# A two-layer decode kernel: the product of probabilities and values with V as the moving operand in four column tiles, its diagonal blocks summed under masks

## The chip, the cores and the metric

The kernel runs on one core of a Trainium2 chip. The metric is the device time of one execution in microseconds (us). Three runs of the kernel before gave 1208.24 us as their median (1208.14 to 1208.75).

## The reference, cut to what matters

Eight sequences (b) of one token each pass through attention, an MLP, the same attention with the same weights and caches, and the same MLP. The caches are read twice, once per layer, since layer 1's queries depend on layer 0's result.

```python
# x [8,1,512]; k_cache, v_cache [8 b, 8 kv heads, 8192 keys, 128]; wq [512,4096]; wo [4096,512]
q = (layernorm(x) @ wq)                       # 32 query heads of 128, four per kv head
scores = einsum("bhqd,bhkd->bhqk", q, k) * 128**-0.5
p = softmax(scores)
o = einsum("bhqk,bhkd->bhqd", p, v)
x = x + o.reshape(8, 1, 4096) @ wo
x = x + silu(layernorm(x) @ w1) @ w2          # w1 [512,1792], w2 [1792,512]
# and the same two blocks once more
```

## The kernel before, in words

**Tasks.** One task is the attention of one layer, one b and one kv head g: 8192 keys and four queries (`REP`). There are 2 x 8 x 8 = 128 tasks, in an order that `make_tasks` (line 141) writes out. Layer 0 of every b comes before layer 1 of the same b. Between them lies a chain of dense work on the token b: output projection, residual, layer norm, MLP, residual, layer norm, query projection for layer 1.

**Granules, halves and positions.** A task has four granules (k = 0 to 3) of 2048 keys, and each granule two halves. A granule of K or V is one load of 512 KB into one of 27 slots of the tile `arena`; partition p holds 16 successive keys, 128 elements each. The program steps through positions p, eight per task (one per half). I call p mod 8 the phase: task i has its scores at positions 8i to 8i+7, its softmax at phases 0 to 7 of the next task's positions, and its PV at positions 8i+13, 15, 17 and 19 (`LP` = 12 positions behind).

**Kept slots.** The last 18 of the 32 (g, k) pairs keep their transposed K in its slot from layer 0 to layer 1 (`KEEP`). In layer 1 the heads g = 4 to 7, and half of g = 3, then load only V. I call these the kept tasks of layer 1. The transposed K of a granule takes the place of K in its slot.

**Loads.** `plan_loads` (line 172) sorts the loads by the position that needs them and gives each a slot and the position after which that slot is free. SP issues them in that order (`issue_until`, line 394; `issue`, line 352; the DMA at line 334), each behind a wait for the PE work that last used the slot. Where slots change hands fastest, in the tasks between the kept ones, a load is issued 7 or 8 positions before it is needed; in the kept tasks of layer 0, 16 to 25 positions.

**One position, in the order in which the program emits it (from line 748).** Every engine executes its own instructions in that order.

- `emit_q` (line 449), once a task: ACT copies the task's queries into QB.
- `emit_t` (line 424): PE transposes the eight 128x128 chunks of the half two positions ahead (line 433). An evacuation copies the result from PSUM back into the slot: three of eight on ACT (line 439), five on DVE (line 441).
- At odd phases `emit_s` (line 458), the scores of the granule: four matmuls with 512 columns each, one in each column tile of 32 (line 464). The queries are the weights and K^T moves. A column tile holds 16 rows in use: four queries times four granules.
- At odd phases `emit_pv` (line 526), both halves of the granule 12 positions back: 16 matmuls with a 128x128 chunk of V as weights and the four columns of P^T, each repeated 12 times, as the moving operand (line 537).
- Softmax. Phase 0: row maxima on DVE (L475), spread onto a diagonal (L477). Phase 1: an fp32 matmul with ones (L485) hands the maxima to all rows; DVE forms the shift (L488, L491), ACT the exponential P and its row sums (L495). Phase 3: sums (L501 on DVE, L504 on POOL). Phase 4: PE transposes P (L513), DVE copies it into PT (L517). Phase 7: reciprocal (L524).
- One or two pieces of the chain, or one head's part of the output projection (`add_heads`, line 709).
- At phase 4, `emit_norm` (line 544, DVE at L551): the task's output times the reciprocal.

PSUM has two banks for scores (SCp), two for PV (OTp), three for transposes (TPp) and one for the dense work (MISC). The bank OTp of a task also takes L485's result.

## Time and profile before

| what | value |
|---|---|
| median of three runs | 1208.24 us |
| the profiled execution's own time | 1207.81 us |
| its span, first to last instruction | 1205.7 us |
| granted TensorE clock, mean | 0.977 |
| PE, DVE, ACT, POOL busy | 981.2, 611.8, 386.1, 70.8 us |
| instructions | 45853, of them 20216 matmuls and 20216 weight loads |
| HBM read | 473.44 MB, 393 GB/s over the span |
| instruction fetches (queues q8 and q14) | 2.61 and 0.32 MB |
| loads of V and K | 512 and 368, 512 KB each |
| issue to landing, median | V 10.7 us, K 15.1 us |

PE is the TensorE, DVE the VectorE, ACT the ScalarE, POOL the GpSimd; SP only issues transfers. The busy time of an engine is an average over stages with different limits, so what counts is the stage: the tables by window show it. "L464" is line 464 of the kernel. In the chain of waits, each step is followed back to what released it; "issue" is time in which the engine waited for nothing that the profile shows. The two microseconds between the execution's time and its span lie outside the first and last instruction.

### The profile page before, as it was taken

How to read it: one execution, taken by the hardware profiler on the slowest of the kernel's cores; microseconds unless marked ns; L12 is line 12 of the kernel's file. 1: busy time of each engine (PE TensorE's matmuls, PEld its weight loads, DVE VectorE, ACT ScalarE, POOL GpSimd, SP SyncE). 2: the span in 40 equal slices, each digit the busy share in tenths (PEclk: the TensorE clock that was granted, in tenths of full speed). 3: DMA queues.
4: the chain of work that ended last, by engine and by line, in shares of the span. 5: the costliest groups of instructions: out<-in, count | busy, mean ns of one | idle time of the engine just before them, and what ended most of it. 6: DMA issues, size and time to landing. Idle time of an engine off the chain costs nothing.

```text
span 1205.7 us, 45853 instructions
## 1 busy us (share of the span) xinstructions
PE 981.2 (81%) x20216; PEld 772.2 (64%) x20216; DVE 611.8 (51%) x1853; ACT 386.1 (32%) x670; POOL 70.8 (6%) x172
## 2 busy tenths in 40 slices
PE   2868898778888788878888898788888898889885
PEld 2656675667666676667666676667666675667564
DVE  2534564446445554546454554446454554456443
ACT  1323332333233332333233332333233333333231
POOL 0000000000000000000000000000000000000000
PEclk7889999999999999999999999999999999999996
DMA  9999999999999999999999999999999999999994
GB/s 370 385 398 408 403 405 406 408 406 399 396 408 408 408 371 404 408 407 403 399 408 407 405 378 408 409 407 395 385 408 407 401 402 407 408 404 398 390 408 172
DMA packets 133926, 476.43 MB, mean 395 GB/s; under 512 B 14160, under 2 KB 20064, under 8 KB 133216
## 3 DMA queue, kind: packets, MB, share of 16 engines
q1 hardware_dynamic: 133728, 473.51, 99.6%
q8 instruction: 159, 2.61, 0.9%
q14 instruction: 39, 0.32, 0.1%
HBM read 473.44 MB, written 0.01 MB: 393 GB/s over the span
## 4 chain that ended last, share of the span: by engine, by line
DMA 47%; PE 32%; DVE 11%; issue 5%; SPq 3%; ACT 2%; POOL 0%; POOLq 0%; ACTq 0%; DVEq 0%
DMA arena<-in_A_k_cache_dram 45%; PE TPp L433 9%; PE OTp L537 9%; PE SCp L464 5%; PE MISC L613 5%; DVE arena L441 3%; SPq L334 3%; DMA arena<-in_A_v_cache_dram 2%; ACT P L495 2%; PE OTp L485 2%; PE TPp L513 1%; DVE rowmax L475 1%; DVE PT L517 1%; PE MISC L631 1%; DVE tr L593 1%
## 5 line engine op out<-in xcount | busy, mean ns | idle before, releaser
L441 DVE COPY arena<-TPp 128x1024 bf16<-128x1024 bf16 x460 | 317.1, 690 | 384.0 <-PE TPp L433 383.6
L433 PE MATMUL TPp<-ident,arena 128*128 128x128 bf16 x5888 | 418.5, 221 | 110.4 <-DMA arena<-in_A_k_cache_dram 92.0
L433 PEld LDWEIGHTS TPp<-ident,arena 128*128 128x128 bf16 x5888 | 341.3, 99 | 129.7 <-DMA arena<-in_A_k_cache_dram 108.9
L439 ACT COPY arena<-TPp 128x1024 bf16<-128x1024 bf16 x276 | 278.7, 1010 | 395.5 <-PE TPp L433 395.4
L537 PEld LDWEIGHTS OTp<-PT,arena 128*128 128x128 bf16 x8192 | 243.1, 96 | 158.7 <-issue 104.5
L537 PE MATMUL OTp<-PT,arena 128*128 128x48 bf16 x8192 | 296.0, 184 | 33.3 <-DVE at L551 9.6
L464 PE MATMUL SCp<-arena,QB 128*32 128x512 bf16 x2048 | 206.8, 394 | 4.9 <-issue 2.1
L495 ACT ACTIVATE P<-SCp,shift 128x512 bf16<-128x512 f32 x128 | 88.0, 687 | 381.7 <-DVE shift L491 261.9
L504 POOL PARTITION_ALL_REDUCE ssa<-ssm x128 | 56.2, 439 | 940.8 <-DVE ssm L501 923.4
L475 DVE TENSOR_REDUCE rowmax<-SCp 128x1 f32<-128x512 f32 x128 | 87.5, 684 | 33.8 <-PE SCp L464 33.8
L464 PEld LDWEIGHTS SCp<-arena,QB 128*32 128x32 bf16 x2048 | 52.9, 93 | 53.0 <-issue 3.3
L485 PE MATMUL OTp<-spread,ones 128*128 128x64 f32 x256 | 55.2, 297 | 28.4 <-DVE spread L477 27.1
L513 PE MATMUL TPp<-ident,P 128*128 128x128 bf16 x512 | 50.0, 220 | 21.9 <-ACT P L495 20.2
L488 DVE SCALAR_TENSOR_TENSOR own<-OTp,real,far 128x64 f32<-128x64 f32 x128 | 36.3, 284 | 53.4 <-PE OTp L485 53.2
L485 PEld LDWEIGHTS OTp<-spread,ones 128*128 128x128 f32 x256 | 38.6, 190 | 36.9 <-DVE spread L477 35.5
L501 DVE TENSOR_SCALAR ssm<-hm,rs 128x4 f32<-128x4 f32 x128 | 28.8, 225 | 42.8 <-ACT P L495 42.8
L513 PEld LDWEIGHTS TPp<-ident,P 128*128 128x128 bf16 x512 | 32.0, 98 | 26.8 <-ACT P L495 23.8
L613 PE MATMUL MISC<-xnT,wq 128*128 128x32 bf16 (+1 forms) x1152 | 38.7, 176 | 4.2 <-issue 2.8
L517 DVE COPY PT<-TPp 128x256 bf16<-128x256 bf16 x128 | 36.4, 285 | 9.6 <-PE TPp L513 9.6
L631 PE MATMUL MISC<-at,wo 128*128 128x32 bf16 (+1 forms) x1152 | 39.9, 175 | 0.3 <-DVE at L551 0.3
L613 PEld LDWEIGHTS MISC<-xnT,wq 128*128 128x128 bf16 x1152 | 35.0, 96 | 5.3 <-issue 3.2
L631 PEld LDWEIGHTS MISC<-at,wo 128*128 128x128 bf16 x1152 | 35.3, 97 | 0.4 <-DVE at L551 0.4
(47 smaller groups left out, 296.3 us busy)
## 6 DMA issues: line engine op xcount, KB each, us to landing
arena<-in_A_v_cache_dram SPq DMA_DIRECT2D x512, 512.0 KB, 10.7
arena<-in_A_k_cache_dram SPq DMA_DIRECT2D x368, 512.0 KB, 15.1
wq<-in_A_wq_dram SPq DMA_DIRECT2D x1, 4096.0 KB, 16.3
wo<-in_A_wo_dram SPq DMA_DIRECT2D x1, 4096.0 KB, 26.5
w<-in_B_w_dram SPq DMA_DIRECT2D x2, 1792.0 KB, 23.1
P<-in_A_x_dram SPq DMA_DIRECT2D x1, 8.0 KB
out_dram<-P SPq DMA_DIRECT2D x1, 8.0 KB
```

The source lines that it names most:

```text
L433: lambda c=c: pe.transpose(tpv[:, c, :], chunk(slot, h * GRP + c), ident[:, :])
L439: op(act, lambda: act.copy(dst, TPp[tb][:, :]), reads=[f"TP{tb}"], writes=[r_half(slot, h)])
L441: op(dve, lambda: dve.tensor_copy(dst, TPp[tb][:, :]), reads=[f"TP{tb}"], writes=[r_half(slot, h)])
L464: lambda c=c: pe.matmul(SCp[bank][c * QUAD:(c + 1) * QUAD, :], QB[qn][:, NGRAN - 1 - k:NGRAN - 1 - k + QUAD], ARENA[:, slot * SLOT + c * K ...
L475: op(dve, lambda: dve.tensor_reduce(rowmax[:, :], SCp[bank][:, :], AX.X, ALU.max), reads=[f"SC{bank}"], writes=["rowmax"])
L485: mm_group([lambda: pe.matmul(every, ones[:, :], spread[:, :], start=True, stop=True)], reads=["ones", "spread"], writes=[f"OT{ob}"])
L495: op(act, lambda: act.activation(P[:, :], SCp[bank][:, :], ACT.Exp, bias=shift[:, 0:1], scale=SM_SCALE, accum_out=rs[st][:, :]), reads=[f" ...
L504: op(pool, lambda: pool.partition_all_reduce(ssa[st][:, :], ssm[st][:, :], 128, bass.bass_isa.ReduceOp.add), reads=[f"ssm{st}"], writes=[f ...
L513: lambda c=c: pe.transpose(tpv[:, c, :], P[:, c * 128:(c + 1) * 128], ident[:, :])
L537: lambda c=c, cc=cc: pe.matmul(otp, chunk(slot, h * GRP + c), pv[:, cc % CPB, cc // CPB % NQ, k, :].unsqueeze(2).to_broadcast([128, REP, P ...
L613: lambda o=o, k=k: pe.matmul(MISC[:, o * n:o * n + w], w_sb[:, k, o * 128:(o + 1) * 128], rhs_of(k).to_broadcast([128, w]) if n == 1 else ...
L631: lambda o=o, h=h: pe.matmul(MISC[:, o * w:(o + 1) * w], wo_sb[:, h, o * 128:(o + 1) * 128], rhs_of(h).to_broadcast([128, w]) if n == 1 el ...
```

## The change

**PV.** V becomes the moving operand. For a granule there are four matmuls, one per column tile c: the weights are the 16 columns of P^T that belong to this tile and granule (four chunks x times four queries r), and the 512 columns of V (four chunks of 128) move. Of the 16 x 512 results of a tile only the four blocks are wanted in which the row's chunk is the column's chunk; the rest is left unused.

**Diagonal.** `emit_diag`, at phase 4 behind the PT copy and the chain's piece: four DVE operations pick the wanted blocks with a mask per row (xm) and sum them over x into a 128x128 fp32 tile, `diag`.

**Pick.** `emit_pick`, at phase 5, right behind the transposes: one fp32 matmul with `diag` as weights and hm (one column per query) moving sums over the rows and turns the result over. `emit_norm` moves to the end of phase 5; the chain of a batch starts one position later.

**Order in a position.** PV now comes before the scores, and both after the softmax and the chain's piece.

**Evacuations.** The first half of a granule goes to ACT and the second to DVE. Where the chain's next piece is heavy on DVE (second, third, fourth, silu) as the first half is emitted, the two are swapped.

**Layouts.** The 16 rows in use of a score tile go by granule and then query; QB, far, hm and PT follow. The tile at2 (layer 1's attention output) takes the place of QT1, with one dependency per b. The two OTp banks are cleared once at the start.

```diff
-PVN = 12
-ACT_EVAC = (1, 4, 7)
...
-    QB = [sb([128, NGRAN - 1 + QUAD], BF16, "QB") for _ in range(NQB)]
+    QB = [sb([128, (NGRAN - 1) * REP + QUAD], BF16, "QB") for _ in range(NQB)]
...
-    at2 = sb([128, HQ, B], BF16, "at2")
+    at2 = QT1
...
-    PT = [sb([128, CPB, NQ * USED], BF16, "PT") for _ in range(NPT)]
+    PT = [sb([128, NQ, NGRAN, CPB * REP], BF16, "PT") for _ in range(NPT)]
...
+    xm = sb([128, CPB], FP32, "xm")
+    diag = sb([128, DH], FP32, "diag")
...
+            for n in range(2):
+                op(dve, lambda n=n: dve.memset(OTp[n][:, :], 0.0), writes=[f"OT{n}"])
...
-                if n % 8 in ACT_EVAC:
+                if h == 0:
+                    turned[0] = bool(chain) and chain[0].__name__ in ("second", "third", "fourth", "silu")
+                if (h == 0) != turned[0]:
                     op(act, lambda: act.copy(dst, TPp[tb][:, :]), reads=[f"TP{tb}"], writes=[r_half(slot, h)])
...
             def emit_pv(i):
                 ti = i // GPT
-                b, g, k, h = where(i)
+                b, g, k, _h = where(i)
...
-                pv = PT[pb][:, :, :].rearrange("p x (c r k) -> p x c k r", c=NQ, k=NGRAN)
-                otp = OTp[ob][:, 0:REP * PVN].rearrange("p (r n) -> p r n", n=PVN)
-                steps = []
-                for c in range(GRP):
-                    cc = (i % GPT) * GRP + c
-                    steps.append(
-                        lambda c=c, cc=cc: pe.matmul(
-                            otp, chunk(slot, h * GRP + c), pv[:, cc % CPB, cc // CPB % NQ, k, :].unsqueeze(2).to_broadcast([128, REP, PVN]),
-                            start=(cc == 0), stop=(cc == NCH - 1),
-                        )
+                steps = [
+                    lambda c=c: pe.matmul(
+                        OTp[ob][c * QUAD:c * QUAD + CPB * REP, :], PT[pb][:, c, k, :],
+                        ARENA[:, slot * SLOT + c * KB:slot * SLOT + (c + 1) * KB],
+                        start=(k == 0), stop=(k == NGRAN - 1),
                     )
-                mm_group(steps, reads=[r_half(slot, h), f"PT{pb}"], writes=[f"OT{ob}"])
+                    for c in range(NQ)
+                ]
+                mm_group(steps, reads=[r_half(slot, 0), r_half(slot, 1), f"PT{pb}"], writes=[f"OT{ob}"])
+
+            def emit_diag(ti):
+                ob = ti % 2
+                for x in range(CPB):
+                    part = OTp[ob][:, x * DH:(x + 1) * DH]
+                    if x == 0:
+                        op(dve, lambda: dve.tensor_scalar(diag[:, :], part, xm[:, 0:1], None, op0=ALU.mult),
+                           reads=[f"OT{ob}", "xm"], writes=["diag"])
+                    else:
+                        op(dve, lambda: dve.scalar_tensor_tensor(
+                            diag[:, :], part, xm[:, x:x + 1], diag[:, :], op0=ALU.mult, op1=ALU.add),
+                           reads=[f"OT{ob}", "xm", "diag"], writes=["diag"])
+
+            def emit_pick(ti):
+                ob = ti % 2
+                mm_group([lambda: pe.matmul(OTp[ob][:, 0:REP], diag[:, :], hm[:, :], start=True, stop=True)],
+                         reads=["diag", "hm"], writes=[f"OT{ob}"])
...
                 emit_t_until(p + LT)
-                if p % GPG == GPG - 1:
-                    if p < NG:
-                        emit_s(p)
-                    for i in range(p - LP - GPG + 1, p - LP + 1):
-                        if 0 <= i < NG:
-                            emit_pv(i)
+                done, late = divmod(p - LP - GPT, GPT)
+                if late == 1 and 0 <= done < ntask:
+                    emit_pick(done)
                 ti, ph = p // GPT - 1, p % GPT
                 if 0 <= ti < ntask and ph in soft:
                     for f in soft[ph]:
                         f(ti)
...
-                done = p - LP - GPT
-                if done >= 0 and done % GPT == 0 and done // GPT < ntask:
-                    tj = done // GPT
-                    emit_norm(tj)
+                if p % GPG == GPG - 1:
+                    if 0 <= p - LP < NG:
+                        emit_pv(p - LP)
+                    if p < NG:
+                        emit_s(p)
+                if late == 0 and 0 <= done < ntask:
+                    emit_diag(done)
+                if late == 1 and 0 <= done < ntask:
+                    emit_norm(done)
```

More of the change, by code (lines that the diff above doesn't have):

```diff
@@ L106, in acquire @@
                 best[k] = t
-        own = self.eng_sem[eng.engine]
+        own = self.eng_sem[self.nc.tensor.engine]
         for t in best.values():
@@ L380, in _ @@
                 lambda: dve.tensor_reduce(
-                    hm[:, :], lanes.rearrange("p c (r k) -> p r c k", k=NGRAN), AX.XY, ALU.add),
+                    hm[:, :], lanes.rearrange("p c (k r) -> p r c k", k=NGRAN), AX.XY, ALU.add),
                 reads=["ident"], writes=["hm"],
             )
+            op(
+                dve,
+                lambda: dve.tensor_reduce(
+                    xm[:, :], lanes.rearrange("p c (x r) -> p x c r", r=REP), AX.XY, ALU.add),
+                reads=["ident"], writes=["xm"],
+            )
+            for n in range(2):
+                op(dve, lambda n=n: dve.memset(OTp[n][:, :], 0.0), writes=[f"OT{n}"])
             op(dve, lambda: dve.tensor_reduce(real[:, :], hm[:, :], AX.X, ALU.add), reads=["hm"], writes=["real"])
@@ L386, in _ @@
                 op(dve, lambda c=c: dve.tensor_scalar(
-                    far[:, c * USED:(c + 1) * USED].rearrange("p (r k) -> p r k", k=NGRAN),
-                    hm[:, :].unsqueeze(2).to_broadcast([128, REP, NGRAN]), real[:, 0:1], -FAR,
+                    far[:, c * USED:(c + 1) * USED].rearrange("p (k r) -> p k r", k=NGRAN),
+                    hm[:, :].unsqueeze(1).to_broadcast([128, NGRAN, REP]), real[:, 0:1], -FAR,
                     op0=ALU.subtract, op1=ALU.mult),
@@ L412, in _ @@
             evacs = [0]
-            tevacs = [0]
             tnext = [0]
+            chain = []
+            turned = [False]
             def has_t(i):
@@ L426, in emit_t @@
                 slot = k_slot[(b, g, k)]
-                n = tevacs[0]
-                tevacs[0] += 1
                 tb = evacs[0] % NTP
@@ L451, in emit_q @@
                 if layer == 0:
-                    q, rq = QT1[:, b * HQ + g * REP:b * HQ + (g + 1) * REP], "QT1"
+                    q, rq = QT1[:, b * HQ + g * REP:b * HQ + (g + 1) * REP], f"QT1_{b}"
                 else:
                     q, rq = QT2[b % 2][:, g * REP:(g + 1) * REP], f"QT2_{b % 2}"
-                qb = QB[ti % NQB][:, NGRAN - 1:NGRAN - 1 + USED].rearrange("p (r k) -> p r k", k=NGRAN)[:, :, 0]
+                qb = QB[ti % NQB][:, USED - REP:USED]
                 op(act, lambda: act.copy(qb, q), reads=[rq], writes=[f"QB{ti % NQB}"])
@@ L464, in emit_s @@
                     lambda c=c: pe.matmul(
-                        SCp[bank][c * QUAD:(c + 1) * QUAD, :], QB[qn][:, NGRAN - 1 - k:NGRAN - 1 - k + QUAD],
+                        SCp[bank][c * QUAD:(c + 1) * QUAD, :], QB[qn][:, USED - (k + 1) * REP:USED - (k + 1) * REP + QUAD],
                         ARENA[:, slot * SLOT + c * KB:slot * SLOT + (c + 1) * KB],
@@ L517, in emit_pt @@
                 op(dve, lambda: dve.tensor_copy(
-                    PT[pb][:, :, :].rearrange("p x (c q) -> p x c q", q=USED),
-                    tpv.rearrange("p x (c q) -> p x c q", q=QUAD)[:, :, :, 0:USED]),
+                    PT[pb][:, :, :, :].rearrange("p c k (x r) -> p x c k r", r=REP),
+                    tpv.rearrange("p x (c q) -> p x c q", q=QUAD)[:, :, :, 0:USED].rearrange(
+                        "p x c (k r) -> p x c k r", r=REP)),
                    reads=[f"TP{tb}"], writes=[f"PT{pb}"])
@@ L549, in emit_norm @@
                 else:
-                    dst, rd = at2[:, g * REP:(g + 1) * REP, b], "at2"
-                op(dve, lambda: dve.tensor_tensor(dst, OTp[ob][:, 0:REP * PVN:PVN], rcp[st][:, :], ALU.mult),
+                    dst, rd = at2[:, b * HQ + g * REP:b * HQ + (g + 1) * REP], f"QT1_{b}"
+                op(dve, lambda: dve.tensor_tensor(dst, OTp[ob][:, 0:REP], rcp[st][:, :], ALU.mult),
                    reads=[f"OT{ob}", f"rcp{st}"], writes=[rd])
@@ L637, in wo_part @@
                         )
-                mm_group(steps, reads=["wo", r_rhs], writes=["MISC"])
+                mm_group(steps, reads=["wo", *r_rhs], writes=["MISC"])
             def add_residual(xnew, rnew, xold, rold, n, w):
@@ L696, in query @@
                         lambda: dve.tensor_copy(dst_of, MISC[:, 0:HQ * n].rearrange("p (h b) -> p h b", b=n)),
-                        reads=["MISC"], writes=[rdst],
+                        reads=["MISC"], writes=rdst,
                     ))
@@ L703, in chain_of @@
                 st += ln_stages(xs[2], "XT2", 1) + settle
-                return st + query(1, QT2[b % 2][:, 0:HQ].rearrange("p (h b) -> p h b", b=1), f"QT2_{b % 2}", QPARTS)
+                return st + query(1, QT2[b % 2][:, 0:HQ].rearrange("p (h b) -> p h b", b=1), [f"QT2_{b % 2}"], QPARTS)
             summed = [0] * (B + 1)
@@ L714, in add_heads @@
                     a = at1[b % 3]
-                    wo_part(g, lambda h: a[:, h:h + 1], f"at1_{b % 3}", 1, first, last)
+                    wo_part(g, lambda h: a[:, h:h + 1], [f"at1_{b % 3}"], 1, first, last)
                 else:
-                    wo_part(g, lambda h: at2[:, h, :], "at2", B, first, last)
+                    wo_part(g, lambda h: at2[:, h:B * HQ:HQ], [f"QT1_{n}" for n in range(B)], B, first, last)
             mm_group(
@@ L735, in _ @@
             soft = {0: [softmax_max], 1: [softmax_shift, softmax_exp], 3: [softmax_sum], 4: [emit_pt], 7: [softmax_rcp]}
-            for f in query(B, QT1[:, 0:B * HQ].rearrange("p (b h) -> p h b", h=HQ), "QT1"):
+            for f in query(B, QT1[:, 0:B * HQ].rearrange("p (b h) -> p h b", h=HQ), [f"QT1_{b}" for b in range(B)]):
                 f()
             emit_q(0)
-            chain = []
             chain_b = [None]
@@ L746, in _ @@
             ntask = len(tasks)
-            for p in range(NG + LP + GPT + 1):
+            for p in range(NG + LP + GPT + 2):
                 tq = (p + LQ) // GPT
@@ L768, in _ @@
                     left = max(1, first1[chain_b[0]] - EARLY - p)
-                    late = len(chain) <= QPARTS or len(chain) > left + QPARTS // 2
-                    for _n in range(2 if late and len(chain) > left else 1):
+                    near = len(chain) <= QPARTS or len(chain) > left + QPARTS // 2
+                    for _n in range(2 if near and len(chain) > left else 1):
                         chain.pop(0)()
@@ L774, in _ @@
                     add_heads(turn[0])
-                done = p - LP - GPT
-                if done >= 0 and done % GPT == 0 and done // GPT < ntask:
-                    tj = done // GPT
-                    emit_norm(tj)
-                    layer, b, _g = tasks[tj]
+                if p % GPG == GPG - 1:
[7 more added lines that the diff above has]
+                    emit_norm(done)
+                    layer, b, _g = tasks[done]
                     if layer == 0:
@@ L783, in _ @@
                         heads[B].append(_g)
-                    if layer == 0 and tj == last0[b]:
+                    if layer == 0 and done == last0[b]:
                         assert not chain and turn[0] == b
```

## The prediction

> **What bounds it now.** I read the page first (slices, chain of waits, groups), then windows of 15 and 5 us, the chain of waits from 410 to 460 us, and the start times of the reduce L475, one in each of the 128 tasks, which give every task its length.

> ```profile
> span 1205.7 us, 45853 instructions
> ...
> DMA  9999999999999999999999999999999999999994
> GB/s 370 385 398 408 403 405 406 408 406 399 396 408 408 408 371 404 408 407 403 399 408 407 405 378 408 409 407 395 385 408 407 401 402 407 408 404 398 390 408 172
> ...
> DMA 47%; PE 32%; DVE 11%; issue 5%; SPq 3%; ACT 2%; POOL 0%; POOLq 0%; ACTq 0%; DVEq 0%
> ```

> The transfers are the bound: a flat top near 408.5 GB/s. 476.43 MB at that rate are 1166.3 us. The rest of the span, from the 5 us windows: 2.9 at the start, 2.5 at 45 to 70 us, about 17 after the last load landed, some 2 scattered, and 14.8 in eight dips. A load (512 KB) takes 1.28 us, a task with K and V (8 loads) 10.28.

> ```profile
> 375.00:390.00 15.00, 12.47 (x256) 10.14 (x253) 6.81 (x19) 6.08 (x11) 0.86 (x2) 1.00 1.03 409
> 420.00:435.00 15.00, 12.31 (x299) 10.48 (x300) 9.31 (x38) 4.92 (x10) 1.21 (x3) 1.00 0.97 371
> 435.00:450.00 15.00, 13.20 (x334) 11.24 (x330) 7.62 (x20) 4.66 (x7) 0.44 (x1) 1.00 0.99 377
> 465.00:480.00 15.00, 13.01 (x271) 9.52 (x268) 7.31 (x23) 3.99 (x9) 0.86 (x2) 1.00 1.03 408
> 1185.00:1200.00 15.00, 6.55 (x172) 5.65 (x171) 4.91 (x26) 1.04 (x3) 1.25 (x3) 0.58 0.22 88
> ```

> Columns: window, its length, busy us of PE, weight loads, DVE, ACT, POOL, granted clock, DMA share, GB/s. At 375 us PE waits for loads; at 420 to 450, where a batch's chain (layer norm, MLP, query) runs between the granules, DMA waits for PE and DVE to free slots: issue to landing falls from 9.6 to 5.5 us. There the tasks take 11.91, 11.52 and 11.93 us. Over the eight chains, three tasks exceed 30.84 us by 1.5, 3.5, 4.5, 2.2, 3.8, 3.8, 1.1, 4.0 (24.4 in all), and the DMA time lost is 0.7, 1.5, 3.1, 1.1, 2.4, 2.8, 1.0, 2.2 (14.8): about 0.65 of the excess. So only those stretches and the tail can move the time; elsewhere the compute has slack.

> ```profile
> 420.75 0.28 DVE PT L517
> 421.03 0.09 DVE at L551
> 421.13 0.05 issue
> 421.18 0.56 PE OTp L537 x16
> ...
> 425.82 1.44 issue
> ...
> 443.91 1.22 issue
> ```

> In the chain of waits of that stretch, DVE leads without a break from 413.45 to 421.13; then PE, with 3.2 us in three gaps that the view calls issue.

> **The change, part by part.** Loads, slots and their order stay.

> ```profile
> L537 PE MATMUL OTp<-PT,arena 128*128 128x48 bf16 x8192 | 296.0, 184 | 33.3 <-DVE at L551 9.6
> L464 PE MATMUL SCp<-arena,QB 128*32 128x512 bf16 x2048 | 206.8, 394 | 4.9 <-issue 2.1
> L485 PE MATMUL OTp<-spread,ones 128*128 128x64 f32 x256 | 55.2, 297 | 28.4 <-DVE spread L477 27.1
> L517 DVE COPY PT<-TPp 128x256 bf16<-128x256 bf16 x128 | 36.4, 285 | 9.6 <-PE TPp L513 9.6
> L488 DVE SCALAR_TENSOR_TENSOR own<-OTp,real,far 128x64 f32<-128x64 f32 x128 | 36.3, 284 | 53.4 <-PE OTp L485 53.2
> L501 DVE TENSOR_SCALAR ssm<-hm,rs 128x4 f32<-128x4 f32 x128 | 28.8, 225 | 42.8 <-ACT P L495 42.8
> ```

> *PV.* 16 pairs a granule, 0.51 us on the chain, become four column-tile matmuls of 512 columns, the shape of the scores: 0.33. I take 0.33, the same shape (bounds: 0.22, the four P transposes of L513 with a quarter of the columns, to 0.55, a score group at 455.20): 4 x 0.18 = 0.72 us saved a task.

> *Pick.* One fp32 matmul a task. L485 is fp32 with the same weights and takes 0.26 on the chain: +0.26.

> *Diagonal.* Four DVE operations on 128x128 fp32 in PSUM, each waiting for the one before. L488 takes 284 ns for 64 columns; L475's 684 for 512 says about 1 ns a column, so some 350 each and 1.5 us with the gaps. Bounds: 0.9 (four of L501) to 2.7 (four of L475).

> *Evacuations.* They go half and half: 92 of 690 ns leave DVE (63 us), 92 of 1010 come to ACT, which is 32% busy. Hidden.

> *Order.* Pick comes after the transposes at phase 5, ahead of PV and scores; PE is in order, so both, and the loads that SP issues behind them, wait for the diagonal. DVE has the diagonal behind the PT copy of phase 4: 0.28 + 1.5 + some 0.15 for the hand-overs, 1.95 us after PT's transposes. PE has 0.45 of transposes in between: a stall of 1.5 us a task. Without a chain a task on PE is then 6.98 of work (8 x 0.45 + 8 x 0.33 + 0.26 + 0.22 + 0.26) and 1.5: 8.5, under 10.28. Hidden by loads; if that cover went, 64 tasks x 1.5.

> *Chain stretch*, by the loop's order with the chain starting a position later. Task one: phase 4 holds the chain's last Newton steps (1.34 us on DVE at 418.91) and an evacuation ahead of the diagonal. From L475 to PV it was 7.1; now 7.1 + 1.5 + 0.2 (residual) to pick, then 3.86 of PE, then transposes and an evacuation ahead of the next L475 (1.24): 13.9 against 11.91. Task two: the same phase holds the variance (0.57), pick stalls 2.45: 11.0 against 11.52. Task three: query matmuls (0.39) shorten the stall to 1.1: 11.2 against 11.93. These have no issue gaps; of 3.2 us I keep 1.2, as PE sends a fifth fewer instructions there (some 1100 for 1380) and the stalls give time to fetch. Sum 37.3 against 35.36: 2.0 more lag a chain, at 0.65 to 1 lost DMA us each; 0.75 gives 8 x 1.5 = **+12**. Bounds: with the short diagonal and no gaps 34.3, a gain of 1; with the long one and all gaps, 43.

> *Kept tasks of layer 1* (V only). There is no transpose to cover: the matmul L485 now stands ahead of PV and scores at phase 1 and waits 1.1 us for L475 and L477, and pick waits 1.95. 3.4 of work and 3.1 of waits: 6.5 a task against 4.86 now. They free two slots per granule, 2.57 us of loads in 1.6 us, so DMA stays fed, and in the five kept tasks of the next batch, whose loads are issued 16 or more positions ahead, PE catches up 10.28 - 8.5 = 1.8 a task: 9 us for 5 x 1.6 = 8 of lag. It fits narrowly. I charge +1.5 in all for queues that refill more slowly after a chain.

> *Tail.* After the last V: PV 0.3 shorter, diagonal 1.5, pick and hand-overs 0.6: **+1.9**, nothing beside it.

> *Instructions.* 16384 PV instructions become 4096, plus 1024: a quarter fewer in all; of 2.93 MB that are fetched 0.75 MB, at 408 GB/s **-1.8**.

> [...]

> **Sum.** 1205.7 + 12 + 1.5 + 1.9 - 1.8 = 1219.3. The profiled run took 1207.8, 2.1 outside its span: 1221.4; the median of the runs is 0.4 higher: **1222 us**.

> **Rivals.**
> *Faster: the shorter PE work decides the chain stretches.* For: PE leads 28 of those 36 us, PV saves 2.2 us per chain, and the issue gaps (3.2) may close. Against: DVE leads the first task already. It decides once the stalls at pick stay under about 4.6 us per chain (2.2 - 0.8 + 3.2), where I count 6.5. With 2 us less lag per chain, 8 x 2 x 0.65 = -10.4, and 1.9 - 1.8: 1195.4, so **1198 us**.
> *Covered.* The dips do as now, the tail and the fetches cancel: **1208 us**. It needs the lag per chain within 0.4 us of today's.
> *PE's clock falls in the kept tasks.* The granted clock was 0.58 where PE was busy 6.55 of 15 us, 1.00 at 12.47; at 453.8 to 456 us a score group took 0.55, PV 0.75. The new kept tasks have PE busy about 4.4 of 6.5 us, between. At 0.55 each kept task grows by 8 x 0.22 = 1.8: five lag 5 x 3.4 = 17, the next five give back 9 and the two tasks ahead of the chain 3.6, so 4.5 are lost in each of seven batches, 31 in all on top of the forecast if every kept task is hit; with three quarters of them, **1245**. [...]
> *It does not do what it says:* column tiles that ran one after another would take four times the 394 ns of L464; four score tiles take 0.33 together, so I give it no weight of its own.

> **Numbers.** Forecast 0.50 (its own range 1212 to 1233), faster 0.28, covered 0.10, clock 0.12. Faster by over 0.2% (2.4 us, about what a measurement of this kernel can tell from no change) 0.28, within 0.08, slower 0.64: a little of the covered case ends on the slow side. Range 1196 to 1247: from the faster rival to the clock's.

> **What would show it.** PE waiting before pick for the diagonal, 1.5 us in plain tasks and over 2 in two of each chain's; the diagonal at 1.4 to 1.6 us; PV at 0.33; plain tasks still 10.2 apart, chain tasks near 14, 11, 11, kept ones 6.5; dips of 3 to 4 us instead of 1.9. Wrong if pick starts without a wait, if the dips shrink, or if plain tasks leave 10.28.

## The result, and the profile after

The changed kernel takes **1328.91 us** as its median (four runs of 1321.23 to 1338.89), beside 1208.19 for the kernel before: a ratio of 1.1004, with a 95% interval of 1.0914 to 1.1093. The forecast was 1222 with a range of 1196 to 1247: the sign was right, and the size 14 us where 121 came. The profile is of the run of 1321.23 us, the fastest of the four, so the stages below account for 113 us.

The page of the changed kernel, the lines that answer to those shown of before:

```profile
span 1319.5 us, 34277 instructions
...
PEclk7979895899679885998679985999589876999676
...
GB/s 377 382 402 408 319 384 409 401 303 346 396 408 325 353 358 409 396 333 301 390 408 324 367 358 409 380 340 334 404 409 317 340 371 409 357 356 325 411 402 4
...
PE 55%; DVE 29%; DMA 10%; issue 4%; ACT 1%; POOL 0%; POOLq 0%; SPq 0%; ACTq 0%; DVEq 0%
```

The flat top of the transfers is gone: every batch has a dip to 300 to 390 GB/s over two or three slices, where before had single slices of 371 to 400. The chain of waits, which was 47% DMA and 32% PE, is now 55% PE, 29% DVE and 10% DMA. The clock's row (PEclk) is low once a batch, where before it was low at the two ends only (7, 8 and 8 in the first three of the 40 slices, 6 in the last, 9 in all between).

Windows of the changed kernel (columns as in the prediction: window, length, PE, weight loads, DVE, ACT, POOL, granted clock, DMA share, GB/s). In this order: kept tasks of layer 1, a chain, the plain tasks of another batch behind its kept ones, the tail.

```profile
360.00:375.00 15.00, 10.31 (x80) 4.43 (x80) 6.02 (x21) 1.64 (x5) 0.86 (x2) 0.50 1.03 409
450.00:465.00 15.00, 12.32 (x214) 9.02 (x206) 6.21 (x21) 5.19 (x9) 1.21 (x3) 0.73 0.81 287
705.00:720.00 15.00, 13.39 (x216) 9.47 (x220) 9.43 (x26) 7.76 (x13) 0.43 (x1) 1.00 0.79 258
1290.00:1305.00 15.00, 8.60 (x102) 4.48 (x99) 7.38 (x25) 1.79 (x3) 0.86 (x2) 0.64 0.01 2
```

The kept tasks have DMA at its full 409 GB/s and PE at **half its clock**; the plain tasks behind such tasks have PE at full clock, busy 13.39 of 15 us, and DMA at 258. The reading is that what the first lose is paid in the second; e1 below tests it.

To see where the time went, I added up, over windows of 5 us, the load time lost against 408.5 GB/s, by the stage that PE was in. "Between" are plain tasks that stand neither ahead of a chain nor behind the kept tasks.

| us of load time lost | before | after | difference |
|---|---|---|---|
| chain (three tasks ahead of the kept ones) | 11.4 | 56.8 | +45.4 |
| kept tasks of layer 1 | 3.3 | 4.0 | +0.7 |
| plain tasks of the next batch behind them | 0.7 | 31.8 | +31.1 |
| between | 1.3 | 32.8 | +31.5 |
| tail (from the last task's row maxima) | 16.7 | 24.9 | +8.2 |
| start | 5.5 | 5.3 | -0.2 |

The differences sum to 116.7; with 0.74 MB fewer fetched (-1.8) that is 114.9, and the span grew by 113.8. In the first and the last batch the chain runs one task earlier than the three ahead of the kept ones; taken where it runs, its row reads 11.2 and 57.0. The prediction's 14.8 counts each dip whole, with what of it falls into the kept tasks. The lengths of tasks (from one row-maximum reduce to the next), as means over the eight chains, and over the seven batches that have a next one:

| us a task | chain | kept, layer 1 | plain, behind them |
|---|---|---|---|
| before | 11.78 10.66 11.44 | 4.87 5.55 4.90 4.87 7.70 | 9.64 10.38 10.45 10.50 10.65 |
| after | 15.49 12.51 11.16 | 7.25 9.60 8.34 8.33 10.14 | 9.20 8.93 9.07 9.05 9.03 |

### The profile page after: what moved, and what is told of

Its sections match the earlier page's. It is cut to its first block, busy times and chain, and to the rows that moved or that the text cites. A ratio compares the mean times of both kernels' runs of the same rounds, so it can differ in the third digit from the quotient of the medians.

```text
span 1319.5 us, 34277 instructions
## 1 busy us (share of the span) xinstructions
PE 983.4 (75%) x14328; PEld 640.7 (49%) x14328; DVE 722.3 (55%) x2276; ACT 479.7 (36%) x762; POOL 70.2 (5%) x172
## 4 chain that ended last, share of the span: by engine, by line
PE 55%; DVE 29%; DMA 10%; issue 4%; ACT 1%; POOL 0%; POOLq 0%; SPq 0%; ACTq 0%; DVEq 0%
PE TPp L440 18%; PE OTp L542 12%; DVE diag L559 10%; PE SCp L473 9%; DMA arena<-in_A_k_cache_dram 9%; DVE rowmax L484 4%; PE MISC L637 4%; PE OTp L565 4%; DVE arena L450 4%; PE OTp L494 3%; PE TPp L522 3%; DVE PT L526 3%; DVE diag L556 2%; PE MISC L655 2%; DVE spread L486 2%
## 5 line engine op out<-in xcount | busy, mean ns | idle before, releaser
L448 ACT COPY arena<-TPp 128x1024 bf16<-128x1024 bf16 x368 | 371.7, 1010 | 474.6 <-PE TPp L440 473.2
L440 PE MATMUL TPp<-ident,arena 128*128 128x128 bf16 x5888 | 440.5, 228 | 35.2 <-DMA arena<-in_A_k_cache_dram 22.8
L450 DVE COPY arena<-TPp 128x1024 bf16<-128x1024 bf16 x368 | 253.2, 688 | 273.7 <-PE TPp L440 273.2
L473 PE MATMUL SCp<-arena,QB 128*32 128x512 bf16 x2048 | 237.8, 456 | 1.6 <-ACT QB L465 1.6
L542 PE MATMUL OTp<-arena,PT 128*16 128x512 bf16 x2048 | 235.4, 452 | 3.7 <-DMA arena<-in_A_v_cache_dram 3.6
L565 PE MATMUL OTp<-hm,diag 128*128 128x4 f32 x256 | 57.7, 295 | 211.6 <-DVE diag L559 194.0
L565 PEld LDWEIGHTS OTp<-hm,diag 128*128 128x128 f32 x256 | 46.4, 227 | 237.4 <-DVE diag L559 218.4
L559 DVE SCALAR_TENSOR_TENSOR diag<-OTp,xm,diag 128x128 f32<-128x128 f32 x384 | 134.7, 351 | 13.6
L484 DVE TENSOR_REDUCE rowmax<-SCp 128x1 f32<-128x512 f32 x128 | 86.9, 679 | 61.5 <-PE SCp L473 61.3
L513 POOL PARTITION_ALL_REDUCE ssa<-ssm x128 | 56.0, 438 | 1126.1 <-DVE ssm L510 992.6
L494 PE MATMUL OTp<-spread,ones 128*128 128x64 f32 x256 | 63.6, 336 | 55.5 <-DVE spread L486 52.0
L494 PEld LDWEIGHTS OTp<-spread,ones 128*128 128x128 f32 x256 | 45.1, 221 | 98.0 <-DVE spread L486 97.9
L542 PEld LDWEIGHTS OTp<-arena,PT 128*16 128x16 bf16 x2048 | 51.2, 91 | 47.5 <-issue 15.2
L497 DVE SCALAR_TENSOR_TENSOR own<-OTp,real,far 128x64 f32<-128x64 f32 x128 | 35.8, 280 | 25.8 <-PE OTp L494 25.8
L556 DVE TENSOR_SCALAR diag<-OTp,xm 128x128 f32<-128x128 f32 x128 | 43.8, 342 | 2.2 <-PE OTp L542 2.2
```

Source lines behind the costliest of these rows:

```text
L440: lambda c=c: pe.transpose(tpv[:, c, :], chunk(slot, h * GRP + c), ident[:, :])
L448: op(act, lambda: act.copy(dst, TPp[tb][:, :]), reads=[f"TP{tb}"], writes=[r_half(slot, h)])
L450: op(dve, lambda: dve.tensor_copy(dst, TPp[tb][:, :]), reads=[f"TP{tb}"], writes=[r_half(slot, h)])
L473: lambda c=c: pe.matmul(SCp[bank][c * QUAD:(c + 1) * QUAD, :], QB[qn][:, USED - (k + 1) * REP:USED - (k + 1) * REP + QUAD], ARENA[:, slot ...
L484: op(dve, lambda: dve.tensor_reduce(rowmax[:, :], SCp[bank][:, :], AX.X, ALU.max), reads=[f"SC{bank}"], writes=["rowmax"])
L494: mm_group([lambda: pe.matmul(every, ones[:, :], spread[:, :], start=True, stop=True)], reads=["ones", "spread"], writes=[f"OT{ob}"])
```

## The experiments

Theory A: the new pauses at pick and at the matmul of the maxima drop PE's clock in the kept tasks, and their lag starves the loads behind them. Theory B: the wait of pick for the diagonal, in every task, is the loss, at whatever clock. AB: both, each in its stage. Each experiment is one execution, only e11 has five; those of the changed kernel lie up to 17.7 us apart, so smaller differences need the stages beside them.

**Dummy matmuls in the kept tasks.** Ten go ahead of pick, five ahead of the matmul of the maxima, into columns of the bank MISC that nobody reads then:

```
+ if lean:  warm(10)      # lean: a kept task; ahead of emit_pick
+ if ph == 1 and lean:  warm(5)
+ pe.matmul(MISC[:, 128:512], ident, w1_sb[:, 0, 0:384], start=False, stop=False)
```

> The changed kernel with PE kept busy in its two pauses of the kept tasks of layer 1: ten matmuls of 384 columns ahead of pick and five ahead of the matmul L494, into columns of MISC that nothing reads. The waits for DVE stay, only the pauses are filled. Theory A (the pauses drop PE's granted clock to 0.5 in those tasks, they take 8.3 us instead of 6.5, PE cannot make up for that before the tasks with tight slots, and DMA starves): granted clock over 0.95 in the mean, kept tasks 6.4 to 7.0 us, a whole of 1250 to 1285 us. Theory B (the waits for the diagonal in every task are the loss, and the low clock only fills time that PE waits anyway): kept tasks stay over 7.8, a whole of 1305 or more.

Measured: 1272.35 us. A window of kept tasks, and the chain of waits of its page:

```profile
345.00:360.00 15.00, 13.26 (x142) 6.59 (x142) 7.51 (x26) 2.37 (x6) 0.86 (x2) 1.00 1.03 409
```

```profile
PE 45%; DVE 30%; DMA 16%; issue 5%; ACT 2%; SPq 1%; POOL 0%; ACTq 0%; POOLq 0%; DVEq 0%
```

With more work on PE the kept tasks go from 8.33 to 6.57 us, at a clock of 1.00. The loss "between" and behind the kept tasks falls from 64.6 to 5.9 us, that in the chain stays (62.7 for 56.8). So A is right for some 50 of the 113 us, and the remaining 64 (1272.35 against 1208) are not the clock of the kept tasks: in the chain 51 more are lost than before the change.

**The order of a position.** Three kernels move lines and change nothing else: pick behind PV and scores (e2); PV and scores ahead of the softmax operations (e3); both (e4).

```
e2: - emit_pick(done)                     # ahead of the softmax operations
    + emit_pick(done)                     # behind emit_pv and emit_s
e3: + emit_pv(p - LP); emit_s(p)          # ahead of the softmax operations
e4: + emit_pv(p - LP); emit_s(p); emit_pick(done)   # all ahead of them
```

> Only pick is moved: from ahead of PV and scores at phase 5 to behind them, so that 0.54 us of PE work covers part of the wait for the diagonal. Theory B: each task loses 0.5 us of stall, plain PE-bound tasks go from 9.0 to 8.5, chain tasks 15.6 and 12.5 to some 15 and 12; 128 tasks less those that DMA bounds, 40 to 60 us: 1265 to 1285. Theory A: the pause only shrinks from 1.8 to about 1.2 us in kept tasks, the clock there stays at 0.5 with tasks of 7.5 to 7.8, and the whole falls by 15 to 45 us: 1280 to 1305; if the clock comes back there, below 1260.

> Only PV and scores are moved ahead of the softmax and the chain's piece, as they were before the change; pick stays where it is. The wait of L494 for the row maxima (1.1 us in kept tasks, 0.2 to 0.4 in plain ones) is then covered. Theory A: one pause of two goes, PE's clock in kept tasks rises above 0.5 for part of the time, tasks of 6 to 7.5 us, a whole of 1260 to 1300. Theory B (pick's wait decides): plain tasks gain 0.2 to 0.4 only, the whole falls by less than 25 us: 1295 or more.

> Both moves: transposes, PV, scores, pick, softmax, chain's piece, diagonal. Theory A: the pauses are under 1 us, the clock stays near 1, kept tasks 5.2 to 6, plain ones about 8.2, and DMA bounds again with dips in the chain tasks: 1205 to 1235. Theory B: each task still waits about 1 us at pick, chain tasks 14 and 12: 1240 to 1265.

Measured: 1247.51, **1346.23** and 1232.17 us. With pick behind PV and scores, PE's wait for the diagonal falls from 194.0 us in all to 79.8, the shortest kept tasks from 8.33 to 7.3, the chain's loss to 44.2, and that "between" and behind the kept tasks from 64.6 to 2.1. The second missed: I had expected a gain. PV and scores ahead of the row maxima leave pick's wait where it was (196.2 us), and the plain tasks behind the kept ones grew to some 10 us, so that nothing was caught up (49.7 us lost there, for 31.8). The clock fell in them too: 0.89 on the mean, where the changed kernel has 0.98. With pick moved too, the same move helps: 25.8 lost in the chain. So the wait at pick mattered more than the one at the maxima. Why the clock of e3's plain tasks fell more often was not tested.

**A quarter of the diagonal.** Three of the four operations are left out (so the output is not the reference's), in the changed kernel's own order:

```
- for x in range(CPB):
+ for x in range(1):
```

> The changed kernel with the first of the diagonal's four DVE operations alone (leaves out three of the four blocks in every output): the price of the diagonal by itself, order as in the change. It is 1.1 us shorter. Theory AB, after e1 and e2 (the waits for the diagonal set the length of every task that DMA does not bound, and their pause also takes the clock away in kept tasks): pick waits 0.3 to 0.5 us in plain tasks instead of 1.35, plain tasks 7.9, kept ones 6 to 7, first chain tasks 14; 1215 to 1245. Rival (the new order of PV, scores and softmax and the even split of the evacuations cost as much by themselves): 1265 or more.

Measured: 1229.93 us; the chain still loses 36.4, the kept tasks take 7.1. Three quarters of the diagonal are worth 91 us (against the profiled run), and yet with a diagonal of 0.34 us the kernel is still 22 us slower than before.

**The old share of evacuations.** The changed kernel with five of eight evacuations on DVE, as before the change:

```
- if (h == 0) != turned[0]:        # ACT: every second one
+ if (tevacs[0] - 1) % 8 in (1, 4, 7):
```

> The changed kernel with the evacuations shared out as before the change (three of eight on ACT, no swap by the chain's pieces). DVE gets 63 us back. Theory AB: DVE is what PE waits for, so the even split helped: 10 to 40 us slower than the change, 1330 to 1365. Rival (ACT, 1010 ns an evacuation and strict in order with the exponential, holds PE up): faster than the change by 10 or more, under 1310.

Measured: **1438.41 us**, far above what was expected. Its waits (total us, times, longest):

```profile
PE OTp L567 <- DVE diag L561: 231.4, 124, 4.1
...
PE OTp L496 <- DVE spread L488: 143.0, 125, 1.2
```

Both of PE's waits for DVE now come in nearly every one of the 128 tasks (the changed kernel has 194.0 us in 120 and 52.0 in 73), and plain tasks take some 10.5 us, longer than their 10.28 of loads. Then no task is left in which anything is caught up. The new share of evacuations, which I had counted as "hidden", is what keeps the change from costing twice as much.

**The kernel before, with only the order changed.** The softmax operations go ahead of scores and PV, as in the changed kernel; the rest stays:

```
+ for f in soft[ph]: f(ti)         # ahead of emit_s and emit_pv
```

> The kernel before with one part of the change alone: softmax and the chain's piece ahead of scores and PV in each position (scores still ahead of PV). In the kept tasks the matmul L485 then waits some 1.0 us for the row maxima with nothing in front of it. By the forecast's reckoning kept tasks grow from 4.86 to 5.6 to 6.0, DMA has backlog there, and the whole moves by 0 to 8 us. If this wait alone takes the clock down (rival), kept tasks are over 6.5 and the whole is 1230 or more.

Measured: 1216.44 us. The order alone costs 8: kept tasks take 4.8 to 6.2 (the last of the five 7.5, before the change 7.7) and keep their clock (0.99), the chain loses 14.0. PE waits 122.0 us for the maxima here, more than in the changed kernel, and this alone takes no clock from the kept tasks.

**The diagonal early.** As e4, and the diagonal right behind the PV that completes the task, ahead of the softmax operations of the same position on DVE:

```
+ if (p - LP - GPT + 1) % GPT == 0:  emit_diag(...)   # behind emit_pv, ahead of emit_pick
```

> e4 (PV, scores and pick ahead of the softmax) with the diagonal moved from the end of phase 4 to phase 3, right behind the task's last PV and ahead of the sums and the chain's piece: DVE then has some 1.9 us of PE work to hide it behind. Theory AB: pick starts without a wait in plain tasks (8.0 or DMA's pace), first chain tasks 12 to 13.5 instead of 14.9, the whole 1200 to 1222. If the chain stretches still lose as much (rival: Newton steps and evacuations on DVE, not the diagonal behind them), within 8 us of e4's 1232.

Measured: 1215.62 us, with the chain's loss at 18.8 and no wait of PE for the diagonal among the longest twenty. The 1.5 us are still spent on DVE; only nobody stands behind them. The clock in the kept tasks is still 0.68, and nothing is lost behind them (0.3).

**The diagonal off DVE, and dummies in e8.** In e9, ACT copies the whole bank to bf16 and pick is four bf16 matmuls with masks of 128x4:

```
- dve.scalar_tensor_tensor(diag, part, xm[:, x:x+1], diag, mult, add)   # x 4
+ act.copy(ocp, OTp[ob])                                       # 128x512, to bf16
- pe.matmul(OTp[ob][:, 0:REP], diag, hm)                       # fp32
+ pe.matmul(OTp[ob][:, 0:REP], ocp[:, x*DH:(x+1)*DH], hmx[:, x*REP:(x+1)*REP])   # x 4
```

> The kernel of e8 (scores, PV, the diagonal behind the last PV and pick, all ahead of the softmax operations of their position), and in it the diagonal leaves DVE: ACT copies the whole output bank (128x512) to bf16 in one operation, and pick becomes four bf16 matmuls with the four 128-column blocks of that copy as weights and the masks, multiplied into 128x4 each, moving. Nothing is left out; the output is rounded to bf16 once before it is normalised. Theory AB (what e8 still loses, 18.8 us of loads in the chain stretches against 11.4 before and some 24 in the tail against 17, is the 1.5 us of diagonal on DVE, which leads in the chain's first task): the chain tasks fall to about 12.5, 11 and 10, their loss to 10-14 us, the tail to about 22, and the time to 1204-1210 us. Rival (PE's work and ACT's evacuations lead there by now; ACT takes some 0.8 us a task more and the first chain task has three of ACT's long operations in a row): the loss moves to ACT, chain loss 17-25, 1212-1222.

> The kernel of e8 with dummy matmuls of 384 columns in the kept tasks of layer 1 alone: three ahead of the fp32 matmul of the row maxima and five ahead of P's transposes, into a bank that is not read then. Nothing is left out. Theory AB (the clock costs time only where the lag of the kept tasks reaches the batch's next tight stretch; in e8 it is caught up, 0.5 and 0.3 us lost there): the kept tasks' clock goes from 0.68 to above 0.9, and the time stays within 1212-1218. Rival A (the clock still costs in e8, through a later start of the chain): the chain's loss falls from 18.8 to under 14 and the time to 1211 or less.

Measured: **1197.39** and 1216.85 us, beside 1208.85 for the kernel before. Dummies in e8 bring the kept tasks to a clock of 1.00 and gain no time: here a low clock cost nothing, since PE was not late for loads behind it. Taking the diagonal from DVE brings the time below what was expected, and the chain's loss to 5.1 (8.1 in the profile of e11), under the 11.4 of before.

**Five rounds, and the same pick in the changed kernel's own order.**

> The kernel of e9 again (one look gave 1197.39 us beside 1208.85 for the kernel before), timed in five rounds: e8's order, the output bank copied to bf16 by ACT, pick as four bf16 matmuls. Theory AB: 1195-1200 us in each round, a ratio to the kernel before of 0.989 to 0.993, the interval wholly under 0.998. Rival (the one look fell well, and the rounds scatter as those of the changed kernel did, 1321 to 1339): a spread over 8 us and an interval that reaches 1.

> The changed kernel with its own order of the program (pick ahead of PV and scores, all behind the softmax operations of their position), and in it only the diagonal replaced as in e9: one ACT copy of the bank and four bf16 matmuls. Nothing is left out. Theory AB with the order as the larger part (PE stands at pick for PT's copy and the copy of the bank whoever does it, and the kept tasks still have their waits in series): kept tasks 6.5 to 7.5 us at a clock under 0.75, chain loss 25-45 us, time 1220-1250. Rival (the four operations on DVE were the loss, and the order is harmless once they are gone): chain loss under 12, time 1196-1206.

Measured: e11 takes 1197.41 us (1197.20 to 1199.74), a ratio to before of **0.9918, 95% interval 0.9904 to 0.9931**: it beats both kernels, the one before by 0.8%. The page of e11, and its rows of the copy and of pick:

```profile
span 1198.0 us, 34751 instructions
...
DMA 51%; PE 26%; DVE 10%; issue 6%; SPq 4%; ACT 2%; POOL 1%; POOLq 0%; ACTq 0%; DVEq 0%
```

```profile
L558 ACT CAST ocp<-OTp 128x512 bf16<-128x512 f32 x128 | 75.3, 588 | 10.0 <-PE OTp L547 9.8
...
L564 PE MATMUL OTp<-hmx,ocp 128*128 128x4 bf16 x512 | 32.7, 168 | 0.7 <-ACT ocp L558 0.7
```

ACT copies all 512 columns in 588 ns, where DVE took four times 350 for 128 each; pick is 128 x 4 short matmuls, and of PE's 194 us of waiting for the diagonal 0.7 are left. Two things changed at once: the engine, and the form, one copy and masks in the matmul in place of four masked sums. The same single copy on DVE was not run; DVE's reduce over the 512 columns of a score bank takes 679 ns (L484 of the changed kernel). DMA leads the chain of waits again, as before the change.

e12 missed. I had held the order for the larger part and expected 1220 to 1250; it takes 1209.44, with 14.4 lost in the chain and 0.8 "between" and behind the kept tasks. So either cure alone removes nearly everything (the order with the early diagonal: 1215.62; ACT: 1209.44), and their gains, 106 and 112 us, don't add up: together they give 124. Beside e5 it also says what about DVE was costly: a diagonal of one operation on DVE loses 36.4 us in the chain, a copy of 588 ns on ACT 14.4 at the same place of the program. So the place in DVE's line counts, and not only the time on it.

**Is the chain's loss the clock too?** In the first task of the chain at 440 us PE stands 3.20 us at pick, and the granted clock is 0.50 from 447.82 to 454.66, 6.84 us in which PE is busy for 5.48. So dummies ahead of pick in the chains as well as in the kept tasks (e13), and in the chains alone (e14):

```
e13: + if lean or chain:  warm(10)     # ahead of emit_pick; and e1's five in the kept tasks
e14: + if chain:  warm(10)
```

> The changed kernel with ten dummy matmuls of 384 columns ahead of pick wherever a chain runs or a task is a kept one, and five ahead of the matmul of the maxima in the kept tasks (e1 had them in the kept tasks alone). Nothing is left out. Theory C (the chain's loss is the clock too: PE works 5.2 and 3.0 us of a chain at half clock, so 4.1 us a chain would go): the three tasks of a chain fall from 39.2 in e1 to some 35.5, the chain's loss from 62.7 to 30-40, time 1240-1252. Rival (DVE's line sets the chain, PE's work behind pick only fills time): the chain's loss stays over 52, time 1262-1280, at a clock of 0.95 or more.

> The changed kernel with ten dummy matmuls ahead of pick in the chains alone; the kept tasks keep their half clock. Nothing is left out. Theory C: the chain's loss falls from 56.8 by some 20-25, and as the batches are less late, that behind the kept tasks by some 10 too: 1285-1300. Rival (DVE's line): within 1315-1335.

Measured: 1261.91 and 1312.07 us. Beside the kernels without them (1272.35 and 1321.23) that is 10 and 9 us; the chain's loss goes from 62.7 to 53.9 and from 56.8 to 48.2, the first task of a chain from 15.83 to 14.83 and from 15.49 to 14.40. Differences in time of that size are not clear of the scatter by themselves; the stages decide. In e14 the chains spend 11 us in all at half clock, in the changed kernel 48, and five of the eight run at full clock throughout. Those five take 37.5 to 37.9 us, where the changed kernel's eight take 38.5 to 40.2, and lose 5.4 us each, beside 7.1 there and 1.4 before. So with the diagonal in its old place most of the chain's loss is there at full clock (the dummies' own time counted in): theory C's 30 to 40 is missed by far. That DVE's line is what is left, e8, e9 and e12 show from the other side.

## Why the prediction was wrong, point by point

**The diagonal: right.** The row of the operation that adds (mean 351 ns; the first one, L556, takes 342), with those of PV and pick:

```profile
L542 PE MATMUL OTp<-arena,PT 128*16 128x512 bf16 x2048 | 235.4, 452 | 3.7 <-DMA arena<-in_A_v_cache_dram 3.6
...
L565 PE MATMUL OTp<-hm,diag 128*128 128x4 f32 x256 | 57.7, 295 | 211.6 <-DVE diag L559 194.0
...
L559 DVE SCALAR_TENSOR_TENSOR diag<-OTp,xm,diag 128x128 f32<-128x128 f32 x384 | 134.7, 351 | 13.6
```

The forecast's 350 had been read off L488 and L475.

**PV cheaper, pick dearer.** On the chain of waits, PV and scores of one granule take 0.54 us together, where the prediction had 0.66, and pick takes 0.39 at full clock, where it had 0.26. The last column of L565's row is PE's wait for the diagonal: 1.35 us in a plain task (forecast 1.5), so this wait was right.

**Plain tasks: hidden, but longer.** 9.03 us, not 8.5. In the chain of waits of one such task (705.08 to 714.11) the sum lacks one head's part of the output projection (0.39), the transposes with the row maxima take 3.61 for 3.15, and the two fp32 matmuls 0.82 for 0.52; PV, scores and the diagonal give 0.6 back. They stay under 10.28, as predicted, but give back 1.25 us each, not 1.8.

**Kept tasks of layer 1: the step that failed.** The prediction costed them at 6.5 us, which is PE at its full clock, and said of the lag that it "fits narrowly". At full clock they do take 6.57 (e1). But the clock was not full, as the timeline of PE at the first kept task of a batch shows (start, duration, operation, and in brackets the pause before it):

```profile
482.34 0.39 PE L473 MATMUL SCp<-arena,QB 128*32 128x512 bf16 x4
483.20 0.40 PE L522 MATMUL TPp<-ident,P 128*128 128x128 bf16 x4 [0.48 <-ACT P L504]
485.40 0.59 PE L565 MATMUL OTp<-hm,diag 128*128 128x4 f32 x2 [1.80 <-DVE diag L559]
485.92 0.60 PE L542 MATMUL OTp<-arena,PT 128*16 128x512 bf16 x4
486.30 0.64 PE L473 MATMUL SCp<-arena,QB 128*32 128x512 bf16 x4
```

The scores take 0.39 us before the pause of 1.80 us and 0.64 behind it. Kept tasks became 8.33, where the rival on the clock had 8.3 (6.5 + 1.8). That rival was held at 0.12, since I took pauses of 1.1 and 1.95 us for too short to cost the clock, which no run had shown. The pauses came as 1.09 and 1.80, and the clock fell all the same. In the profiles of before and after the granted clock changes only after whole multiples of 3.41 us, and these are the three steps around that fall (columns as in the windows above):

```profile
478.54:481.96 3.42, 3.22 (x54) 2.35 (x54) 2.30 (x6) 2.12 (x3) 0.00 (x0) 1.00 0.92 321
481.96:485.37 3.41, 1.16 (x20) 0.38 (x12) 2.17 (x8) 0.86 (x3) 0.44 (x1) 1.00 0.98 338
485.37:488.78 3.41, 2.40 (x18) 0.92 (x18) 1.14 (x4) 0.00 (x0) 0.00 (x0) 0.50 1.00 398
```

In the second PE is busy 1.16 of 3.41 us; in the third the granted clock is 0.50. The clock falls eleven times in the changed kernel's kept tasks: each time PE was busy for 0.34 to 0.47 of the step of 3.41 us ahead of the fall, and no pause in these tasks is over 1.80 us. So here a fall goes with the work in a step, and judging by one pause at a time is what kept the rival small.

The rival's own sum was too small too. Five kept tasks grew by 43.7 - 27.9 = 15.8 us a batch (it had 17), but the next five give back 5 x 10.28 - 45.3 = 6.1, not 9 and then 3.6. What is left, 9.7 in each of seven batches, is 68; measured are 62.6 ("between" and behind the kept tasks), of which e1 takes away 58.7.

**Chain: the mechanism was right, the clock was not in it.** Of the chain that the prediction worked out, the tasks took 15.85, 13.19 and 11.01 us against a forecast of 13.9, 11.0 and 11.2 (and 1.2 of gaps): a lag of 4.7 more than before, not 2.0. The chain of waits in its first task, whose row maxima began at 440.27:

```profile
445.58 0.69 DVE arena L450
446.28 0.20 DVE PT L526
446.47 0.08 DVE tr L616
...
447.72 0.26 DVE diag L556
...
449.18 0.59 PE OTp L565 x2
449.77 0.53 PE OTp L542 x3
...
450.73 0.97 PE TPp L440 x8
```

DVE has an evacuation, PT's copy, the last Newton steps and the diagonal in one line of 3.6 us, and PE stands before pick for 3.2 of it. Pick itself is on time: 8.9 us after the row maxima, forecast 8.8; and so, nearly, are the stalls at pick in the other two tasks, 2.19 and 0.95 us (2.45 and 1.1). What comes behind pick is not: 6.9 us to the next row maxima, forecast 5.1, with PE's rows 1.5 to 1.7 times as long (0.59, 0.53 and 0.97 here; 0.39, 0.32 and 0.57 at full clock). The same happens at 458 us in the second task. So the chain too was priced at full clock. This is that chain before the change, after it, and in e14, where it keeps its clock (columns as above):

```profile
414.06:449.42 35.36, 29.54 (x694) 24.68 (x690) 21.28 (x80) 11.69 (x19) 2.93 (x7) 1.00 0.99 380
440.27:480.32 40.05, 30.97 (x557) 22.77 (x556) 23.16 (x89) 14.94 (x22) 2.87 (x7) 0.87 0.91 332
437.38:474.86 37.48, 32.51 (x587) 23.64 (x586) 23.19 (x88) 14.95 (x22) 2.87 (x7) 1.00 0.96 350
```

At full clock it takes 37.48 us for a forecast of 37.3. That is in part luck: its first task takes 13.96 (forecast 13.9), but its second 12.11 for 11.0, with a wait of PE for the row maxima of 1.23 us that the sum did not have, and the 1.2 us of gaps kept for the whole chain happen to make up for it. So of the 4.7 us some 2.1 are the forecast's own lag and some 2.6 the clock.

The second error is the share that is lost. 0.65 of the excess over the loads' 30.84 us had been read off a kernel whose queue refills in every plain task. Counted in the same way, the eight chains exceed 30.84 by 66.5 us (24.3 before), which is 5.3 more lag a chain, and lose 57.0 (11.2 before): 1.1 us for each us of added lag, where the forecast took 0.75. So +45 for +12. That the share is higher because the kernel comes late to its chains is argued, not tested by itself.

**The rival that was faster** was to decide once the stalls at pick stay under 4.6 us a chain; they are 6.3 (3.20, 2.19, 0.95), so it fell by its own condition. Once the reduction is off DVE and out of the way, e11 gives 1197.4, where that rival had 1198; that is another kernel, and the nearness says nothing for the rival's sum.

**Tail: the term right, its cover gone.** From the last row maxima to the end it takes 25.1 us for 22.9: +2.2, forecast +1.9. The other 6 of the +8.2 are loads that before the change still arrived in the tail, and here had landed ahead of it, because PE was late by then.

**Instructions: right.** 0.74 MB fewer are fetched (0.75 forecast).

**What stays open.** Where exactly the clock falls: the steps of 3.41 us bound it (last section), but between 0.4 and 0.7 of a step busy the same share is followed by a fall or not. How much of the gain of e9 and e12 is the engine and how much the form of the reduction. And why a us of lag costs 1.1 us of loads here.

## What to carry to other kernels

A wait that is hidden in the plain stage must be priced again in the stage with the least work: there it is uncovered, and PE's clock can be lower there as well (0.50 in the kept tasks here), so that the work around it is dearer (8.33 us a task, for 6.57 at a clock of 1.00 in e1). A lag is harmless only while the next stage can give all of it back, so sum the lag and the return over a whole batch, at the measured task length and not at the sum of parts. And when a result has to be reduced in the middle of the path, take the engine whose line is short: at the same place of the program the changed kernel is 113 us slower than before with the reduction on DVE, and 2 with it on ACT.

## What the runs showed of the hardware that was not expected

```profile
459.56 0.43 PE L499 MATMUL OTp<-spread,ones 128*128 128x64 f32 x2 [1.09 <-DVE spread L491]
...
461.50 0.40 PE L527 MATMUL TPp<-ident,P 128*128 128x128 bf16 x4 [0.53 <-ACT P L509]
...
462.37 0.61 PE L547 MATMUL OTp<-arena,PT 128*16 128x512 bf16 x4
```

- A bank of 512 fp32 columns takes ACT 588 ns to copy to bf16 (e11); four masked passes of 128 columns take DVE 4 x 350, and one pass over 512 columns, the reduce of the row maxima, 679.
